# Moving four small loads from GpSimd's queue to ScalarE's, and draining GpSimd after each expert's outputs, in a gated linear attention with a routed mixture of experts

## The chip, the cores and the metric

The kernel runs on one core of one Trainium2 chip. The metric is device time in microseconds (us) of one execution, as the median of several executions. The engines are PE (TensorE), DVE (VectorE), ACT (ScalarE), POOL (GpSimd) and SP (SyncE). Each has an instruction stream of its own, and SP, ACT and POOL can also issue transfers (DMAs). In the views, "SPq" or "ACTq" is the instruction sequencer of that engine; a busy time is that of the engine itself, and the issuing of DMAs isn't counted in it.

## The reference

Two blocks follow each other. The first is a linear attention with complex gates: 4 batches, 8 heads, 768 steps, head width 48.

```python
mag = np.sqrt(a_re * a_re + a_im * a_im)
scale = np.minimum(mag, 0.999) / (mag + 1e-06)
a_re_n, a_im_n = (a_re * scale, a_im * scale)
for t in range(S):
    ar, ai = (a_re_n[:, :, t, :, None], a_im_n[:, :, t, :, None])
    new_re = ar * S_re - ai * S_im
    new_im = ar * S_im + ai * S_re
    kv = np.einsum('bhd,bhe->bhde', k[:, :, t], v[:, :, t])
    S_re, S_im = (new_re + kv, new_im)
    y[:, :, t] = np.einsum('bhd,bhde->bhe', q[:, :, t], S_re)
```

Its result, seen as 3072 tokens of width 384, goes through a router that picks one of 8 experts (hidden width 1024) for each token.

```python
logits = x @ w_gate
expert_idx = np.argmax(logits, axis=1)
...
for e in range(E):
    mask = expert_idx == e
    xe = x[mask]
    h = np.maximum(xe @ w1[e], 0.0)
    ye = h @ w2[e]
    out[mask] = gate_w[mask, None] * ye
```

## The kernel before

**Set-up.** POOL writes constants: the identity, counters, masks, and the tile `across` (line 231), which is cleared with a memset (line 232). Then four small DMAs on POOL's queue put the router's weights `w_gate` into parts of `across` (lines 235 and 236), and two POOL copies put identity blocks into other parts of it (line 237). POOL goes on with memsets of the unused rows of the tiles `st`, `xf`, `KX` and `QX`. PE multiplies by `across` at the end of each attention step, to turn the output and add the router's logits in one matmul.

**The gates.** For each batch the gates come in four pieces of four steps (`JQ`), as two DMAs each, real part and imaginary part, into the tile `big0`. So SP's queue begins with eight loads of 288 KB, in the order re, im, re, im and so on. For each piece the function `limit` (lines 405 to 437) applies the magnitude limit: ACT squares both parts (`Square`, line 414), DVE or PE adds them, ACT takes the logarithm and the exponential, and so on; ACT and DVE take turns, each waiting for the other's result. The function `front` then runs the recurrence on DVE, `fix` and `fold` make decayed queries and keys, and `attention` does the matmuls.

**The order.** All of this is first written as operations with costs. A planner (`in_time`) sorts them, and they are emitted in that order through `InOrder`, a wrapper that makes an engine keep the order in which the program was written. `P`, `V`, `A`, `T` and `Q` are such wrappers of POOL, DVE, ACT, PE and SP. ACT's stream begins with an activation-table load (line 294), a copy into `notes`, and the first `Square`.

**Completion semaphores.** Each DMA of SP or ACT signals on one of eight completion semaphores, which the framework gives out in turn in program order, whichever of the two queues issues it. A DMA that gets a semaphore again waits for the DMA that had it before. The first eight are those of the eight gate loads. POOL's DMAs have eight of their own.

**Routing.** After each batch the rows of x are written by indirect DMAs on POOL (line 788) into the DRAM buffer `sorted_x`, sorted by expert.

**The experts.** The loop of lines 894 to 937 goes over the eight experts. For each it loads up to 448 rows, multiplies by `w1` (24 matmuls), applies ReLU on ACT and DVE alternately, multiplies by `w2`, scales each block of 128 rows by its gate into a tile `yo` (three buffers), and the last 64 rows into `yh` (two buffers). The function `to_out` (lines 268 to 273) writes each with an indirect DMA on POOL into `out`: three blocks `yo` and one `yh` for most experts. The weights of expert e + 3 are fetched on SP's queue (line 933).

Of the kernel before, what the change touches and what calls it, by code (L numbers as in the profile page):

```python
# [17 lines left out]
B, H, S, D = 4, 8, 768, 48  # L18
N, DM, E, F = B * S, H * D, 8, 1024
# [13 lines left out]
XW = R2 + E  # L33
# [106 lines left out]
def gateloop_then_moe(ctx, tc, q, k, a_re, a_im, v, wg, w1, w2, out):  # L140
    nc = tc.nc
# [9 lines left out]
    def bc(ap, shape):  # L151
        return ap.to_broadcast(shape)
# [4 lines left out]
    def stt(o, a, s, b, op0, op1):  # L157
        nc.vector.scalar_tensor_tensor(out=o, in0=a, scalar=s, in1=b, op0=op0, op1=op1)
# [5 lines left out]
    P = InOrder(tc, nc.gpsimd)  # L164
# [6 lines left out]
    def blocks(e, u, a, z):  # L171

        return sorted_x[e * N + a:e * N + z, x_at(u)[0]:x_at(u)[0] + R2].rearrange("(c j) w -> j c w", j=32)
# [57 lines left out]
    across = consts.tile([128, H // 4, XW + E], FP32, name="across")  # L231
    P.memset(across, 0.0)
    for u in range(2):
        for n in range(2):
            P.dma_start(across[u * 64:u * 64 + D, :, (0 if n else XW):(E if n else XW + E)],
                        wg.rearrange("(m n u d) e -> u n d m e", n=2, u=2, d=D)[u, n])
        P.tensor_copy(across[u * 64:u * 64 + D, :, E + u * D:E + u * D + D],
                      bc(ident[u * 64:u * 64 + D, None, u * 64:u * 64 + D], [D, H // 4, D]))

# [20 lines left out]
    def fetch(e, queue):  # L260
        for w, at, n in ((w1, 0, DT * F), (w2, DT * F, FT * DM)):
            queue.dma_start(big[e % 3][:, at:at + n], w[e * 128:e * 128 + 128])

    def weights(e):
        w = big[e % 3]
        return w[:, 0:DT * F].rearrange("p (d f) -> p d f", f=F), w[:, DT * F:DT * F + FT * DM].rearrange("p (f d) -> p f d", d=DM)

    def to_out(y, rows, index):
        move = nc.gpsimd.indirect_dma_start(out=rows, out_offset=bass.IndirectOffsetOnAxis(ap=index, axis=0), in_=y,  # L269
                                            in_offset=None, bounds_check=rows.shape[0] - 1, oob_is_err=False).ins  # L270
        for other in outs:
            tc.declare_no_dep(move, other, reason="each token has a row of its own")
        outs.append(move)
# [17 lines left out]
    with ExitStack() as att:  # L291
# [401 lines left out]
        def early(weights_in):  # L693
# [28 lines left out]
            for i in range(EARLY // 128):  # L722
                o_ps, wait = (two[:, 0:DM], readers[0]) if i else (ps[7][:, 0:DM], used["at", 2])
                for f in range(FT):
                    o = pe(DM / 600 / 0.111, lambda i=i, f=f, o_ps=o_ps: T.matmul(o_ps, lhsT=ht[f][:, i * 128:i * 128 + 128], rhs=w2t[:, f, :],
                                                                                  start=(f == 0), stop=(f == FT - 1)),
                           [hts[f]] + ([o] if f else []), wait, first=B * G)
                o = act(DM, lambda i=i, o_ps=o_ps: A.activation(ys[i], o_ps, func=ACT.Copy, scale=gt_e[:, i, 0:1]), [o, state["early notes"]], free)
                pool_dma(1.1, lambda i=i: to_out(ys[i], out, to_e[:, i:i + 1]), [o, to])
# [122 lines left out]
    with ExitStack() as ms:  # L852
        xp = ms.enter_context(tc.tile_pool(name="xp", bufs=2))
        T = InOrder(tc, nc.tensor)
        TT, HALF = CAP // 128, DM // 2

        def notes_of(e):

            r = e * N
            gt = xp.tile([128, TT + 1, 2], FP32, name="gt")  # L860
            nc.sync.dma_start(gt[:, 0:TT, :], sorted_x[r:r + TT * 128, XD:].rearrange("(t p) w -> p t w", p=128))
            for u in range(2):
                nc.sync.dma_start(gt[u * 64:u * 64 + 64, TT, :], sorted_x[r + TT * 128:r + CAP, XD:])
            return gt

        def load(e):

            xq = xp.tile([128, CAP // 32, R2], FP32, name="xq")
            c0 = first_tile(e) * 4
            for u in range(4):  # L870
                nc.sync.dma_start(xq[u * 32:u * 32 + 32, c0:], blocks(e, u, c0 * 32, CAP))
            return xq, notes_of(e)

        def first_tile(e):
            return EARLY // 128 if e == 0 else 0

        def bank_of(kind):
            own = {"h": (2, 3, 4, 5), "o": (6, 7)}[kind]
            turn[kind] = turn.get(kind, -1) + 1
            return ps[own[turn[kind] % len(own)]]  # L880
        turn = {}

        def turned(e, xq):

            xt = mp.tile([128, DT, CAP], FP32, name="xt")
            for d in range(DT):
                c0 = first_tile(e) * 4
                nc.vector.transpose(xt[:, d, c0 * 32:].rearrange("p (c j) -> p c j", j=32), xq[:, c0:, d * 32:d * 32 + 32])  # L888
            return xt

        xq, gt = load(0)
        mp = ms.enter_context(tc.tile_pool(name="mp", bufs=2))
        xt = turned(0, xq)
        for e in range(E):
            if e + 1 < E:
                xq, gt_next = load(e + 1)
            w1t, w2t = weights(e)
            to = mp.tile([128, TT + 1], I32, name="to")
            t0 = first_tile(e)
            nc.vector.tensor_copy(to[:, t0:TT], gt[:, t0:TT, 1])  # L900
            stt(to[:, TT:TT + 1], gt[:, TT, 1:2], 2.0, upper, ALU.mult, ALU.add)
            ht = mp.tile([128, FT, CAP], FP32, name="ht")
            for f in range(FT):
                cols = slice(t0 * 128, CAP)
                h = bank_of("h")[:, cols]
                for d in range(DT):
                    T.matmul(h, lhsT=w1t[:, d, f * 128:f * 128 + 128], rhs=xt[:, d, cols], start=(d == 0), stop=(d == DT - 1))
                if f % 2:
                    nc.vector.tensor_scalar_max(ht[:, f, cols], h, 0.0)  # L909
                else:  # L910
                    nc.scalar.activation(ht[:, f, cols], h, func=ACT.Relu)  # L911
            if e + 1 < E:
                xt = turned(e + 1, xq)
            for i in range(t0, TT):
                o = bank_of("o")[:, 0:DM]
                for f in range(FT):
                    T.matmul(o, lhsT=ht[:, f, i * 128:i * 128 + 128], rhs=w2t[:, f, :], start=(f == 0), stop=(f == FT - 1))
                y = mp.tile([128, DM], FP32, name="yo", bufs=3)
                if i % 2:
                    nc.vector.tensor_scalar_mul(y, o, gt[:, i, 0:1])  # L920
                else:
                    nc.scalar.activation(y, o, func=ACT.Copy, scale=gt[:, i, 0:1])  # L922
                to_out(y, out, to[:, i:i + 1])
            o = bank_of("o")[:, 0:DM]
            for f in range(FT):
                for u in range(2):
                    T.matmul(o[u * 64:u * 64 + 64, 0:HALF], lhsT=ht[:, f, TT * 128:CAP], rhs=w2t[:, f, u * HALF:u * HALF + HALF],
                             start=(f == 0), stop=(f == FT - 1))
            y = mp.tile([128, HALF], FP32, name="yh", bufs=2)
            nc.vector.tensor_scalar_mul(y, o[:, 0:HALF], gt[:, TT, 0:1])  # L930
            to_out(y, halves, to[:, TT:TT + 1])
            if e + 3 < E:
                fetch(e + 3, nc.sync)
            if e == E - 2:
                n_gen = nc.values_load(trips[0:1, 0:1], min_val=0, max_val=1, skip_runtime_bounds_check_because="0 or 1")  # L935
            if e + 1 < E:
                gt = gt_next
# [176 lines left out]
```

## Time and profile before

| what | value |
|---|---|
| median of 5 executions | 665.64 us (664.05 to 668.29) |
| the profiled execution | 665.01 us, of which the span from first to last instruction is 663.3 us |
| PE busy | 548.9 us (83%) |
| DVE busy | 368.8 us (56%) |
| ACT busy | 289.5 us (44%) |
| POOL busy | 78.7 us (12%) |
| granted PE clock | 0.928 |

The span covers the instructions; the profiled execution's own time is 1.7 us longer. Shares of the whole span are averages over stages: the attention takes about the first 365 us, the experts the rest.

### The profile page before, as it was taken

The page shows a single profiled execution, that of the slowest core. Times are in us where ns is not written, and L with a number is a line of the kernel's source. Part 1 is how long each engine was busy: PE and PEld are TensorE (multiplying, and loading weights), DVE is VectorE, ACT ScalarE, POOL GpSimd, SP SyncE. Part 2 cuts the span into 40 slices and gives each one's busy share as a digit, 9 for nine tenths or more (in the row PEclk, how much of TensorE's full clock was granted, in tenths as well). Part 3 has the DMA queues.
Part 4 walks back from the last instruction along what each step waited for, and adds up shares of the span by engine and source line. Part 5 has one row for each costly group of instructions (what it writes and reads, how often), then busy time and mean ns, then how long its engine had stood idle before and what let it go on. Part 6 is the DMA issues. An engine that isn't in the chain of part 4 may idle for free. (4 is left out here: it accounts for less than half of the span.)

```text
span 663.3 us, 8204 instructions
## 1 busy us (share of the span) xinstructions
PE 548.9 (83%) x2594; PEld 336.2 (51%) x2594; DVE 368.8 (56%) x782; ACT 289.5 (44%) x940; POOL 78.7 (12%) x96
## 2 busy tenths in 40 slices
PE   1541388968899588968998999999999999999993
PEld 0220245645565355645566675555555555655552
DVE  5999999999999999999735121111111202010100
ACT  6555588688998688767743111010110100010100
POOL 9100000000004005003102110111101020101111
PEclk9865599989999588988999999999999999999998
DMA  9694856276724656078479434454554440100000
GB/s 258 151 247 116 193 161 175 79 194 163 192 70 125 185 153 183 29 180 203 113 274 398 89 132 121 139 141 138 151 139 136 116 126 30 37 6 24 9 12 29
DMA packets 77635, 89.81 MB, mean 135 GB/s; under 512 B 25341, under 2 KB 67343, under 8 KB 75536
## 3 DMA queue, kind: packets, MB, share of 16 engines
q1 hardware_dynamic: 74000, 79.33, 44.1%
q0 software_dynamic: 3584, 9.87, 4.2%
q8 instruction: 22, 0.36, 0.2%
q14 instruction: 29, 0.24, 0.1%
HBM read 54.31 MB, written 16.63 MB: 107 GB/s over the span
## 5 line engine op out<-in xcount | busy, mean ns | idle before, releaser
L136 PE MATMUL bank<-xt,big 128*128 128x448 f32 (+1 forms) x384 | 136.1, 515 | 1.1 <-DVE xt L888 1.1
L136 PE MATMUL bank<-big,ht 128*128 128x384 f32 (+1 forms) x608 | 136.8, 420 | 0.0
L136 PE MATMUL bank<-QX,KX 128*128 128x224 f32 (+1 forms) x384 | 96.0, 383 | 35.3 <-ACT QX L136 29.9
L136 PEld LDWEIGHTS bank<-big,ht 128*128 128x128 f32 (+1 forms) x608 | 84.7, 168 | 53.5 <-issue 6.9
L136 PEld LDWEIGHTS bank<-xt,big 128*128 128x128 f32 x384 | 71.3, 190 | 63.1 <-issue 60.8
L136 PEld LDWEIGHTS bank<-QX,KX 128*128 128x128 f32 x384 | 69.9, 209 | 52.0 <-issue 34.3
L909 DVE TENSOR_SCALAR ht<-bank 128x448 f32<-128x448 f32 (+1 forms) x32 | 18.9, 591 | 103.6 <-PE bank L136 103.6
L136 ACT ACTIVATE big<-big 128x576 f32<-128x576 f32 (+3 forms) x77 | 68.5, 902 | 15.5 <-DVE big L136 14.2
L136 ACT ACTIVATE QX<-diag,KX 96x48 f32<-96x48 f32 x280 | 72.4, 334 | 2.7 <-DMA KX<-pk 2.7
L911 ACT ACTIVATE ht<-bank 128x448 f32<-128x448 f32 (+1 forms) x32 | 16.5, 517 | 121.8 <-PE bank L136 121.8
L136 PE MATMUL two<-big,ident 128*128 128x512 f32 (+1 forms) x112 | 42.8, 538 | 29.7 <-ACT big L136 25.6
L788 POOL DMA_INDIRECT sorted_x<-xf,slot x24 | 29.8, 1242 | 316.6 <-DMA big<-in_a_im_dram 154.5
L136 PE MATMUL bank<-ak,vb 128*48 128x224 f32 (+1 forms) x384 | 54.2, 366 | 14.4 <-ACT ak L136 12.1
L136 DVE TENSOR_TENSOR big<-big,big 128x576 f32<-128x576 f32 (+3 forms) x86 | 65.0, 767 | 1.0 <-ACT big L136 0.2
L922 ACT ACTIVATE yo<-bank,gt 128x384 f32<-128x384 f32 x15 | 8.7, 580 | 122.4 <-PE bank L136 122.4
L136 DVE TENSOR_TENSOR big<-big 128x288 f32<-128x288 f32 (+5 forms) x108 | 55.2, 519 | 6.1 <-ACT big L136 5.3
L136 DVE TENSOR_TENSOR ak<-bank,causal 128x256 f32<-128x256 f32 x96 | 40.0, 419 | 17.1 <-PE bank L136 16.7
L269 POOL DMA_INDIRECT out_dram<-yo,to x22 | 21.3, 970 | 230.2 <-ACT yo L922 184.9
L136 PEld LDWEIGHTS two<-big,ident 128*128 128x128 f32 x112 | 22.6, 237 | 49.6 <-issue 32.6
L136 PE MATMUL bank<-QX,st 128*48 128x224 f32 (+1 forms) x320 | 43.5, 351 | 0.8 <-ACT st L136 0.8
L136 PE MATMUL bank<-across,ys 128*128 128x104 f32 x192 | 38.3, 291 | 4.7 <-ACT xf L136 2.3
L136 DVE TENSOR_TENSOR big<-big,carry 128x672 f32<-128x672 f32 x48 | 39.2, 853 | 0.1
(126 smaller groups left out, 548.7 us busy)
## 6 DMA issues: line engine op xcount, KB each, us to landing
big<-in_moe_w_dram SPq DMA_DIRECT2D x16, 1536.0 KB, 6.6
KX<-pk SPq DMA_DIRECT2D x44, 146.2 KB, 3.9
QX<-pk SPq DMA_DIRECT2D x44, 144.0 KB, 3.6
sorted_x<-xf SPq DMA_DIRECT2D x8, 731.5 KB, 6.5
xq<-sorted_x SPq DMA_DIRECT2D x28, 168.0 KB, 7.7
big<-in_a_re_dram SPq DMA_DIRECT2D x16, 288.0 KB, 3.3
big<-in_a_im_dram SPq DMA_DIRECT2D x16, 288.0 KB, 3.9
qt<-in_q_dram SPq DMA_DIRECT2D x12, 384.0 KB, 5.0
```

Source lines behind the costliest of these rows:

```text
L136: return lambda *a, **kw: self.tc.keep_in_program_order(f(*a, **kw))
L269: move = nc.gpsimd.indirect_dma_start(out=rows, out_offset=bass.IndirectOffsetOnAxis(ap=index, axis=0), in_=y, in_offset=None, bounds_chec ...
L788: move = nc.gpsimd.indirect_dma_start(out=sorted_x[:, :], out_offset=bass.IndirectOffsetOnAxis(ap=slot[:, i:i + 1], axis=0), in_=xfs[(b * ...
L909: nc.vector.tensor_scalar_max(ht[:, f, cols], h, 0.0)
L911: nc.scalar.activation(ht[:, f, cols], h, func=ACT.Relu)
L922: nc.scalar.activation(y, o, func=ACT.Copy, scale=gt[:, i, 0:1])
```

## The change

Two edits. The four loads of `w_gate` into `across` move from POOL's queue to ACT's, where they stand ahead of everything else that ACT does. And POOL gets a `drain` instruction behind the `yh` output of each of the experts 0 to 6. The outputs are now issued through `P`, so they keep program order on POOL.

```diff
@@ -232,8 +232,8 @@
     P.memset(across, 0.0)
     for u in range(2):
         for n in range(2):
-            P.dma_start(across[u * 64:u * 64 + D, :, (0 if n else XW):(E if n else XW + E)],
-                        wg.rearrange("(m n u d) e -> u n d m e", n=2, u=2, d=D)[u, n])
+            nc.scalar.dma_start(across[u * 64:u * 64 + D, :, (0 if n else XW):(E if n else XW + E)],
+                                wg.rearrange("(m n u d) e -> u n d m e", n=2, u=2, d=D)[u, n])
         P.tensor_copy(across[u * 64:u * 64 + D, :, E + u * D:E + u * D + D],
                       bc(ident[u * 64:u * 64 + D, None, u * 64:u * 64 + D], [D, H // 4, D]))
@@ -266,8 +266,8 @@
     def to_out(y, rows, index):
-        move = nc.gpsimd.indirect_dma_start(out=rows, out_offset=bass.IndirectOffsetOnAxis(ap=index, axis=0), in_=y,
-                                            in_offset=None, bounds_check=rows.shape[0] - 1, oob_is_err=False).ins
+        move = P.indirect_dma_start(out=rows, out_offset=bass.IndirectOffsetOnAxis(ap=index, axis=0), in_=y,
+                                    in_offset=None, bounds_check=rows.shape[0] - 1, oob_is_err=False).ins
@@ -929,6 +929,9 @@
             to_out(y, halves, to[:, TT:TT + 1])
+            if e < E - 1:
+
+                P.drain()
             if e + 3 < E:
                 fetch(e + 3, nc.sync)
```

The built program shows what this does to the instruction streams. The order of the work of PE, DVE, SP and POOL, and of ACT behind its first instructions, is as before. POOL's stream has the seven drains, with no wait of their own. ACT's stream now begins as follows, where each wait is for the completion semaphore of one of the eight gate loads, or for POOL's memset of `across`:

```
ACT 1  DMA across<-w_gate   waits for gate load 2 (im) and POOL's memset of across
ACT 2  DMA across<-w_gate   waits for gate load 4 (im)
ACT 3  DMA across<-w_gate   waits for gate load 5 (re)
ACT 4  DMA across<-w_gate   waits for gate load 7 (re)
ACT 5  activation-table load
ACT 6  copy into notes
ACT 7  Square of gate piece 1 (waits for gate load 1)
```

Before, instructions 5, 6 and 7 were the first three, and `Square` waited for the gate loads 1 and 2. On SP's queue the DMAs behind the gate loads have other completion semaphores than before, and so other earlier DMAs to wait for: the load of `kt_in` waits for gate load 3, the first of the six loads of `vb` for gate load 6 and the second for gate load 8 (before: 2, 3 and 4).

## The prediction

> **What bounds the kernel now.** I read first the table of busy time by stage, because shares of the whole span hide which engine is late where. Columns: stage, its length, then busy time and instruction count of PE, PE's weight loads, DVE, ACT and POOL, then granted clock, DMA share and GB/s.
>
> ```profile
> 0.00:16.60 16.60, 3.21 (x4) 1.50 (x5) 9.88 (x30) 10.59 (x16) 15.18 (x38) 1.00 0.91 258
> 100.00:200.00 100.00, 85.79 (x544) 56.53 (x541) 98.19 (x184) 87.93 (x307) 1.43 (x1) 0.97 0.56 147
> 200.00:300.00 100.00, 78.69 (x487) 51.25 (x486) 97.01 (x207) 76.27 (x281) 15.51 (x11) 0.86 0.52 141
> 400.00:663.00 263.00, 252.44 (x889) 141.23 (x888) 35.57 (x72) 22.98 (x42) 27.16 (x28) 0.99 0.29 82
> ```
>
> From about 100 to 300 us DVE has no room (98.19 and 97.01 of 100 us); among the experts PE has none (252.44 of 263). POOL is nowhere late, except that it is busy with memsets at the start. The first 16.6 us are different: no compute engine is full, so there a chain of waits sets the pace. So next I read ACT's timeline of the first 9 us (start, length, instruction, idle time before it and what ended that).
>
> ```profile
> 0.83 1.28 ACT L136 ACT_TABLE_LOAD   x1 [0.83 <-PEq L1103]
> 3.62 0.20 ACT L136 COPY notes<-token 128x6 f32<-128x6 f32 x1 [1.51 <-DVE token L219]
> 4.78 1.16 ACT L136 ACTIVATE big<-big 128x1152 f32<-128x1152 f32 x1 [0.96 <-DMA big<-in_a_im_dram]
> 6.77 0.77 ACT L136 ACTIVATE big<-big,w_bias 128x576 f32<-128x576 f32 x1 [0.82 <-DVE big L136]
> ```
>
> The first `Square` starts at 4.78, the moment gate load 2 is there. DVE's first use of it follows: DVE sits idle 2.24 us until `ACT big`, and starts at 5.98. After that ACT and DVE wait only for each other and for PE: among ACT's waits of the first 60 us the one of 1.0 us above is the only one on a DMA. So everything on ACT, DVE and PE behind it hangs on that 4.78.
>
> Third, SP's timeline of the same stretch, for the gate loads, and the DMA view taken around the issues of load 2 and of load 7 (last number: us from issue to landing).
>
> ```profile
> 1.34 0.49 SPq L136 DMA_DIRECT2D big<-in_a_im_dram  x1
> 2.42 0.51 SPq L136 DMA_DIRECT2D big<-in_a_im_dram  x1
> 2.97 0.51 SPq L136 DMA_DIRECT2D big<-in_a_re_dram  x1
> 4.36 1.78 SPq L136 DMA_DIRECT2D big<-in_a_re_dram  x1
> ```
>
> ```profile
> big<-in_a_im_dram SPq DMA_DIRECT2D x1, 288.0 KB, 3.4
> ```
>
> ```profile
> big<-in_a_re_dram SPq DMA_DIRECT2D x1, 288.0 KB, 6.7
> ```
>
> Load 2 landed at 1.34 + 3.4 = 4.7, which fits 4.78. Load 7 is issued at 4.36 and landed at 4.36 + 6.7 = 11.1. The loads between have no landing in this view; they were issued sooner.
>
> **The change, part by part.** *ACT's loads.* ACT now holds four DMAs ahead of its table load, and each waits on ACT's own stream. The first waits for load 2 (4.7; the memset of `across` ended at 3.17 + 0.33 = 3.5), the second and third for loads 4 and 5, the fourth for load 7: 11.1. Behind them stand the table load, the copy and the first `Square`, and so DVE's and PE's first work. The sum for the new start of `Square`:
> - fourth DMA may start at 11.1 (only this wait counts; loads 4 and 5 were issued 1.9 and 1.4 us before load 7, and their DMAs fit in between);
> - its issue: no DMA on ACT's queue is in the trace. Nearest rows: SP's gate loads take 0.45 to 1.78 us, median about 0.5; SP's small loads of `gt`, which have as few bytes, 0.49 to 2.83 with a median of 0.60; POOL's four loads of `across` themselves 0.56 to 0.79. I take 0.55, with 0.45 and 1.8 as ends. An issue at nothing isn't excluded either; it would take 0.55 off;
> - the table load 1.28, which before lay under the wait for `token` and cost nothing; that cover is gone;
> - the copy 0.20, of which I count 0.15, as ACT instructions overlap a little (the one at 8.88 takes 0.19 and the next starts at 8.97), and 0.1 for two hand-overs (4.7 to 4.78 is one).
>
> 11.1 + 0.55 + 1.28 + 0.15 + 0.1 = 13.2, against 4.78: **8.4 us later**. With 1.8 for the issue it is 9.6; with the issue at nothing, 7.8. Between the table load and the next ACT instruction the trace shows 1.51 us idle, given to `token`; the end of that wait (3.37 + 0.23 = 3.60) explains the next start. So any time that ACT needs behind a table load is bounded by 0 and 1.51, and the trace can't say more. I take 0, because the named releaser fits to 0.02 us, and keep 1.51 for the range: up to 11.1 in all.
>
> The Trainium skill ("ScalarE: Activation LUTs", section "What ACT_TABLE_LOAD costs") gives 1283 ns for the load, which this trace shows too, and puts a drain of 1380 ns behind it. By that rule the sum would be an estimated 9.8 us; no row here shows such a drain.
>
> *What the delay meets later.* A late start is made up only if some engine on the path waits, later, for something whose time does not hang on the first `Square`. Such things are the loads of q, k and v (SP issues them by 12.5, DVE multiplies by `qt` first at 63.5), the zeroing by POOL (its last memset starts at 18.1, first needed with the first `QX` at 64) and the `across` loads (PE first reads `across` at 85.8). All have 40 us and more to spare. Their cover is not touched: SP's loads of `kt_in` and `vb` now wait for other gate loads, at the latest load 8, issued at 6.18; even 4 us more leaves them 40 us early, and none of SP's later gate loads goes ahead of ACT's and DVE's progress anyway (the next one starts at 19.50). So I carry the whole 8.4 us to the end: at 98% busy DVE can't catch up.
>
> *What POOL saves.* Four DMA issues, 0.56 to 0.79 us each and about 2.5 us in all, so its memsets end about 2.7 us sooner. Nothing waits for them: 0.
>
> *Drains.* POOL's timeline among the experts:
>
> ```profile
> 470.83 0.97 POOL L269 DMA_INDIRECT out_dram<-yh,to  x1 [1.58 <-DVE yh L930]
> 494.43 0.97 POOL L269 DMA_INDIRECT out_dram<-yo,to  x1 [22.63 <-ACT yo L922]
> ```
>
> ```profile
> out_dram<-yh,to POOLq DMA_INDIRECT x8, 6.7
> ```
>
> A drain stands behind `yh`, and behind it the next expert's first `yo` is queued, which comes 22.6 us after. No drain is in the trace. Its bounds: nothing if it only waits for POOL's own pipe, and the landing of the output (6.7 us median, 9.9 the longest of all outputs) if it waits for that. A gain is excluded as it takes no work away. Even 9.9 leaves 12 us. So each of the seven costs 0; without the cover it would be up to 7 x 6.7 = 47 us. The last expert's outputs, which end the kernel, have none. `P` instead of the bare engine changes no order on POOL.
>
> The sum is made on the profiled execution: 665.01 + 8.4 = 673.4. That execution is 0.63 us under the median, so I forecast 665.64 + 8.4 = **674.0 us**.
>
> A second rule speaks the other way on the transfer itself: the skill ("DMA: Bandwidth & Descriptors", section "Issuing engine by pattern") sends simple loads to the hardware queues of SP or ACT, as generally faster than GpSimd's. By that rule alone the change would cost nothing, since these loads (5.0 us from issue to landing on POOL) are not waited for: 665.6. The row that decides is not the transfer's speed but what stands behind it on ACT.
>
> **The rivals.**
> - *Larger on ACT* (chance 0.2): the issue stalls as SP's did for load 7 (1.78), or ACT needs the 1.51 us behind the table load. 9.6 to 11.1 us later: 675.2 to 676.7. For it: SP's issue did stall just then, with eight loads on the way. Against it: by 11.1 seven of the eight have landed.
> - *Made up later, not slower* (0.08): ACT's late start is taken up by idle time in the opening of the attention. The place is the stretch 0 to 16.6, where DVE is busy only 9.88 and ACT 10.59 us; with all gate pieces landed, the two might overlap more. It decides if DVE reaches the end of `front` at the old time, for which DVE must win 8.4 us out of 6.7 idle ones. Then 665.6 us. Against it: those gaps are each other's results, in a fixed order, and no later gate load was waited for.
> - *Relieved POOL* (0.03): the memsets end 2.7 us sooner and something did wait for them: 663 at best, if ACT's waits cost nothing. No row shows such a waiter.
> - *Drains wait and are met* (0.04): POOL held up for more than 22.6 us behind a drain. From there each further us costs up to seven, 1 us over giving 681. The longest landing of an output is 9.9.
>
> **How the numbers follow.** My forecast case has 0.65 and gives 672.5 to 675: 7.8 to 8.4 us more, and about 1 us for the spread of medians, estimated from single executions between 664.05 and 668.29. The range takes in the larger case with half of that spread, up to 677.2; down to 671.2 it takes in a landing of load 7 that is 2 us sooner in other executions, and the spread. Left out are the last three cases, 0.15. A measurement of this kernel tells from no change about 0.5%, or 3.3 us: slower means over 669. The forecast, the larger case and the drains make 0.89 slower; made up later is the 0.08 of no difference; 0.03 remain for faster.
>
> **What would show it.** Right: in the changed profile ACT's table load starts near 11.7 instead of 0.83, the first `Square` near 13.2, DVE's first use of it near 14.4, and the same offset of about 8 us is seen in `qt`'s first use (63.5 before), in the first `yo` output (394.1) and at the end; POOL's gap before a `yo` stays near 22.6. Wrong: the offset shrinks on the way (then something absorbs it), the table load starts early, the four DMAs don't wait in order, or a `yo` output starts later than its data.

## The result, and the profile after

With both edits the kernel takes 668.4 us (median of 33 executions, 665.32 to 670.07), against 665.62 us before (59 executions): 2.8 us more, a ratio of 1.0036 (95% interval 1.0027 to 1.0045). The forecast was 674.0 us. The direction was right; the size was three times too large, and the time lies below the range. The profiled execution took 669.75 us, its span is 668.1 us.

ACT's timeline at the start, with the same columns as before:

```profile
4.73 6.00 ACTq L235 DMA_DIRECT2D across<-in_moe_w_gate_dram  x4
10.77 1.28 ACT L136 ACT_TABLE_LOAD   x1 [10.77 <-DMA big<-in_a_re_dram]
12.06 0.20 ACT L136 COPY notes<-token 128x6 f32<-128x6 f32 x1
12.16 1.16 ACT L136 ACTIVATE big<-big 128x1152 f32<-128x1152 f32 x1
```

The four loads hold ACT's sequencer from 4.73 to 10.73; the table load is released by a real part of the gates, which is load 7. The DMA view around the issue of load 7 (at 4.07) shows its landing 6.3 us later, at 10.4, and the view of line 235 shows what one issue costs on ACT's queue (min, median and max in ns):

```profile
big<-in_a_re_dram SPq DMA_DIRECT2D x1, 288.0 KB, 6.3
```

```profile
L235 ACTq DMA_DIRECT2D across<-in_moe_w_gate_dram x4: 318/318/394, 4.7 to 10.4; - x4
```

So `Square` starts at 12.16 instead of 4.78: 7.4 us late. Nothing makes that up on the way. The last `yh` on DVE, with which the computing ends, is at 652.48 before and at 661.79 after:

```profile
652.48 0.42 DVE L930 TENSOR_SCALAR yh<-bank,gt 128x192 f32<-128x192 f32 x1 [7.30 <-PE bank L136]
```

```profile
661.79 0.42 DVE L930 TENSOR_SCALAR yh<-bank,gt 128x192 f32<-128x192 f32 x1 [7.30 <-PE bank L136]
```

That is 9.3 us late, but the span is only 4.8 us longer. From this instruction to the end it is 10.8 us before and 6.3 us after: the kernel gained 4.5 us in its last 11 us. POOL's timeline before, which I had read, ends with the last output:

```profile
653.18 0.97 POOL L269 DMA_INDIRECT out_dram<-yh,to  x1 [1.58 <-DVE yh L930]
```

That is at 654.15, and the span ends at 663.3. My prediction took no account of the 9.2 us between. The view of the program's last line, under which its closing instructions stand, shows it, first before, then after (count, min/median/max in ns, first and last start):

```profile
L1110 POOLq DRAIN  x3: 46/108/4972, 657.5 to 663.0; - x3
```

```profile
L1113 POOLq DRAIN  x3: 46/103/378, 666.8 to 667.8; - x3
```

The long one of the three drains is the first; "the last drain" below is this one. Every program here ends with it. It took 4.97 us before, from 657.5 to 662.5, and takes 0.38 us after, 4.6 us less. The core's end waits for it: in the same view before, the next instructions of POOL's and of SP's sequencer start behind it.

```profile
L1110 POOLq EVENT_SEMAPHORE  x4: 17/17/17, 662.5 to 663.2; - x4
L1110 SPq EVENT_SEMAPHORE  x2: 17/17/17, 662.6 to 663.3; - x2
```

The seven new drains are in the view of POOL's other instructions, between 390 us and the end:

```profile
L136 POOLq DRAIN  x7: 2531/8918/10457, 405.8 to 625.8; - x7
```

They take 2.5 to 10.5 us each, and POOL's timeline shows that no output is late for them: the gap before the next `yo` is 22.62 us, before it was 22.63.

```profile
443.68 0.98 POOL L136 DMA_INDIRECT out_dram<-yh,to  x1 [1.57 <-DVE yh L930]
467.27 0.98 POOL L136 DMA_INDIRECT out_dram<-yo,to  x1 [22.62 <-ACT yo L922]
```

7.4 - 4.6 = 2.8 us is just what the medians show (the interval of the ratio is 1.8 to 3.0 us). The two profiles alone differ by 4.8 us, because between the first `Square` and the last `yh` one took 647.7 us and the other 649.6. In the ten profiles of this document the stretch takes 647.3 to 649.8 us, and short and long ones stand in both groups of kernels, with and without drains. So it goes with neither edit and looks like spread between executions; with one profile of each kernel that can't be shown.

### The profile page after: what moved, and what is told of

The parts are those of the page before. It is cut to its first block, busy times and chain, and to the rows that moved or that the text cites. A ratio compares the mean times of both kernels' runs of the same rounds, so it can differ in the third digit from the quotient of the medians.

```text
span 668.1 us, 8205 instructions
## 1 busy us (share of the span) xinstructions
PE 552.1 (83%) x2594; PEld 337.1 (50%) x2594; DVE 369.0 (55%) x782; ACT 289.2 (43%) x940; POOL 76.9 (12%) x92
## 5 line engine op out<-in xcount | busy, mean ns | idle before, releaser
L136 PE MATMUL two<-big,ident 128*128 128x512 f32 (+1 forms) x112 | 44.7, 556 | 37.0 <-ACT big L136 32.9
L136 PEld LDWEIGHTS bank<-across,ys 128*128 128x128 f32 x192 | 31.8, 207 | 15.5 <-ACT xf L136 4.8
```

What stands on the lines that cost most here:

```text
L136: return lambda *a, **kw: self.tc.keep_in_program_order(f(*a, **kw))
```

## The experiments

Theory: ACT's late start costs its full 7.4 us, and the drains take the work of the last drain to a place where POOL is idle. The main rival: the late start is mostly made up on the way, and the drains do nothing. Eight kernels were run, each in five rounds beside the kernel before, whose median was 665.59 us beside the first four and 665.96 us beside the others. The cuts of code are against the kernel before; those of the two kernels with one drain, and of the drain behind every output, are against the kernel with the drains alone, and that of the loads on SP against the changed kernel. `...` stands for what is left out.

**The loads on ACT alone**

```diff
-            P.dma_start(across[...], wg...)
+            nc.scalar.dma_start(across[...], wg...)
```

> Only the first edit: the four loads of across on ACT's queue, no drains. Theory A (ACT's late start costs its full 7.4 us, and the drains take about 4.6 us off the last drain of the program): first Square near 12.2 us as in the changed kernel, the program's last drain near 4.6 us (56 DMAs of POOL stand before it instead of 60), time 7.4 us over before, about 673.0. Rival B (ACT's late start is mostly made up in the attention, drains do nothing): 2 to 3 us over before, about 668.4, as with both edits.

Measured 671.95 us, a ratio of 1.0104 (1.0077 to 1.0131), which is 6.4 us between the medians and 6.9 by the ratio. In its profile `Square` starts at 11.81, 7.0 us late. The last drain:

```profile
L1110 POOLq DRAIN  x3: 40/103/4651, 664.1 to 669.4; - x3
```

4.65 us against the 0.05 + 56 x 0.082 = 4.64 expected. The time is 1.0 us under the expected 673.0: `Square` was 7.0 us late and not 7.4, and the sum had left out that the last drain gets 0.3 us shorter, which leaves 6.7. So the start is lost in full, as far as the interval tells (5.1 to 8.7 us); the rival, 668.4, falls.

**The drains alone**

```diff
-        move = nc.gpsimd.indirect_dma_start(...)
+        move = P.indirect_dma_start(...)
...
+            if e < E - 1:
+                P.drain()
```

> Only the second edit: the seven drains, the loads of across on POOL as before. Theory A: first Square at 4.8 us, the last drain 0.4 us instead of 4.97, time 4.6 us under before, about 661.0. Rival B (drains do nothing): 665.6, and a last drain near 5 us. Rival C (the shorter tail comes from the loads that left POOL's queue): the same 665.6.

Measured 660.58 us, a ratio of 0.9939 (0.9916 to 0.9962), 5.0 us between the medians. `Square` is at 4.95, the last drain takes 0.37 us:

```profile
L1113 POOLq DRAIN  x3: 46/108/373, 657.6 to 658.6; - x3
```

So the drains are worth about the 4.6 us that the last drain lost (4.1 by the ratio), and both rivals, at 665.6, fall. The two edits add up: +1.04% and -0.61% make +0.43%, and both together measured +0.36%.

**One drain, behind expert 6**

```diff
-            if e < E - 1:
+            if e == E - 2:
                 P.drain()
```

> Loads on POOL, one drain alone, behind the outputs of expert 6. If what a drain clears is counted in POOL's DMAs since the last drain (theory A1: 0.05 us + 0.082 us for each, from 4.97 us behind 60 and 0.38 behind 4): last drain 0.4 us, time 661.0 as with seven drains; the one inner drain takes at least 0.05 + 56 x 0.082 = 4.6 us. If it needs all seven (A2, each drain clears only its own share): last drain well over 2 us, time over 663.

Measured 660.59 us, 0.9924 (0.9899 to 0.9949). One drain does what seven do; A2 falls. The views of the inner and of the last drain:

```profile
L136 POOLq DRAIN  x1: 5855/5855/5855, 618.6 to 618.6; - x1
```

```profile
L1112 POOLq DRAIN  x3: 46/108/378, 659.6 to 660.6; - x3
```

The one inner drain takes 5.86 us, above the lower bound of 4.6.

**One drain, behind expert 0**

```diff
-            if e < E - 1:
+            if e == 0:
                 P.drain()
```

> Loads on POOL, one drain alone, behind the outputs of expert 0, so 28 DMAs of POOL follow until the last drain. Theory A1 (a price for each DMA since the last drain): last drain 0.05 + 28 x 0.082 = 2.35 us, time 2.6 us under before, about 663.0. Rival A3 (any earlier drain does all of it, as a first-use cost): last drain 0.4 us, 661.0.

Measured 664.09 us, 0.9965 (0.9943 to 0.9986); by the ratio 2.3 us less than before, by the medians 1.5. The last drain is the sharper reading:

```profile
L1112 POOLq DRAIN  x3: 46/108/2338, 659.8 to 662.7; - x3
```

2.34 us against 2.35 expected. So the last drain is not a first-use cost. It has a price for each DMA of POOL since the drain before. The outputs go through `P` here too, so it is the place of the drain that counts and not this wrapper.

**The table load ahead of the loads on ACT**

```diff
+    A0 = InOrder(tc, nc.scalar)
+    A0.preload_act_table_set("natural_log_exp_and_others")
...
-            P.dma_start(across[...], wg...)
+            A0.dma_start(across[...], wg...)
...
-        A.preload_act_table_set("natural_log_exp_and_others")
```

> The first edit alone, but with the activation-table load ahead of the four loads on ACT, where it lies under the wait for gate load 2. Theory A (the delay is a sum of the wait for gate load 7, one issue of 0.32, the uncovered table load of 1.28 and the copy): first Square near 10.8 us instead of 12.0, time 5.9 to 6.1 us over before, about 671.6; the last drain 4.64 us behind 56 DMAs. Rival (time beyond the table load's own 1.28 us stands behind it): the gain is 2.6 us, Square near 9.4.

Measured 671.32 us, 1.0083 (1.0070 to 1.0096). In the timeline the table load is back under the wait, and `Square` starts at 10.20:

```profile
0.83 1.28 ACT L136 ACT_TABLE_LOAD   x1 [0.83 <-PEq L1104]
4.83 5.22 ACTq L136 DMA_DIRECT2D across<-in_moe_w_gate_dram  x4
10.09 0.20 ACT L136 COPY notes<-token 128x6 f32<-128x6 f32 x1 [7.98 <-DMA big<-in_a_re_dram]
10.20 1.16 ACT L136 ACTIVATE big<-big 128x1152 f32<-128x1152 f32 x1
```

1.61 us sooner than with the loads alone. 1.28 of it is the table load; ACT's loads ended 0.33 sooner here (10.05 against 10.38). The rival's 2.6 isn't there. Over the kernel before beside each, the loads alone took 6.4 us more and this kernel 5.4, by the medians (6.9 and 5.5 by the ratios); the intervals overlap, so the times don't confirm the 1.28.

**One load of four on ACT**

```diff
-            P.dma_start(across[...], wg...)
+            (P if u or n else nc.scalar).dma_start(across[...], wg...)
```

> The first of the four loads on ACT, the other three on POOL, no drains. It waits only for gate load 2, which the first Square waits for in any case. Theory A (the waits for the later gate loads are the main price, not ACT's queue): first Square near 4.7 + 0.32 + 1.28 + 0.1 = 6.4 us, time 1.6 us over before, about 667.2. Rival D (a load on ACT's queue costs by itself, each a quarter of 7.4): about 1.9 from the queue plus the uncovered table load, Square near 8.0, 668.8. Last drain 0.05 + 59 x 0.082 = 4.9 us.

Measured 667.33 us, 1.0021 (1.0008 to 1.0033), 1.4 us between medians. ACT's timeline:

```profile
4.84 0.39 ACTq L235 DMA_DIRECT2D across<-in_moe_w_gate_dram  x1
5.26 1.28 ACT L136 ACT_TABLE_LOAD   x1 [5.26 <-DMA big<-in_a_im_dram]
6.66 1.16 ACT L136 ACTIVATE big<-big 128x1152 f32<-128x1152 f32 x1
```

`Square` starts at 6.66: the wait for load 2, which it has anyway, then one issue and the table load. So a load on ACT's queue costs little by itself; the waits for later gate loads make most of the 7.4. The last drain takes 4.89 us behind 59 DMAs (4.9 expected).

**The loads on SP, with the drains**

```diff
-            nc.scalar.dma_start(across[...], wg...)
+            nc.sync.dma_start(across[...], wg...)
```

> The loads of across on SP's queue, behind the gate loads and the load of qt; the seven drains as in the change. Theory A: nothing that is needed soon stands behind them on SP, so first Square at 4.8 us, last drain 0.4 us, time as with the drains alone, 660.6. Rival (the four waits on SP hold up loads that matter): over 662.

Measured 661.05 us, 0.9927 (0.9914 to 0.9941). `Square` at 4.86, last drain 0.38 us. SP's timeline has the four loads behind the load of `qt`:

```profile
7.79 1.78 SPq L235 DMA_DIRECT2D across<-in_moe_w_gate_dram  x4
```

They are issued in one run, from 7.79 to 9.57, so no wait held them up for long there. They cost nothing that the times can tell, and what stands behind them on SP isn't needed for some 50 us. Which of the two spares the time, the short waits or what stands behind, this run doesn't separate.

**A drain behind every output of experts 0 to 6**

```diff
                 to_out(y, out, to[:, i:i + 1])
+                if e < E - 1:
+                    P.drain()
```

> Loads on POOL; a drain behind every output of experts 0 to 6, those behind a yo followed by the next output 2.6 to 5.2 us later, so the cover is much smaller. If a drain ends about 0.2 us after the landing of the output before it (theory A, landings of yo about 2.6 us): the yh output of each expert starts up to 0.6 us late, nothing on PE waits for it, time as with seven drains, 660.6. If drains hold POOL longer than the gaps: yo buffers run out, PE waits, over 662.

Measured 660.91 us, 0.9928 (0.9915 to 0.9941). The time is as expected, but the drains are longer than I thought. POOL's timeline of one expert:

```profile
431.97 0.97 POOL L136 DMA_INDIRECT out_dram<-yo,to  x1 [4.20 <-ACT yo L922]
436.67 0.97 POOL L136 DMA_INDIRECT out_dram<-yh,to  x1 [3.74 <-issue]
```

The `yh` output starts after 3.74 us of idle time instead of 1.58, so 2.2 us late and not 0.6. PE doesn't wait for it: 20.48 us of idle time follow before the next `yo` (at 458.12). On DVE the small copies of line 900 do wait longer for outputs to land, 9.6 us in two places against 2.9 in one before, but DVE has room among the experts.

The quickest kernels are those with a drain behind expert 6 and without loads on ACT, 660.6 to 661.1 us; the runs don't separate them. They beat both the kernel before and the changed one.

## Why the prediction was right or wrong

**What bounds the kernel: right at the start, blind at the end.** The first `Square` does set the pace of all that follows. But I read the stages by busy time, which counts no drain, and so took the 9.2 us behind the last output as nothing.

**ACT's loads: right in mechanism, a little large.** The order, the waits and the end of the table load's cover were as I said. Forecast 8.4 us, measured 7.4. Load 7 landed at 10.4 instead of 11.1 (it was issued 0.3 us sooner and took 0.4 less), an issue took 0.32 instead of 0.55, and the copy with its hand-overs took 0.1 less than the 0.25 that I had put down. The issue was faster than every one of the rows I took as bounds (0.45 to 2.83), but within the bound of nothing that I had kept.

**The time behind a table load: 0 was right.** The copy starts at 12.06, and the load ends at 10.77 + 1.28 = 12.05. The 1380 ns of drain that the Trainium skill ("ScalarE: Activation LUTs", section "What ACT_TABLE_LOAD costs") puts behind it are not there; the measurement decides. The same page's 1283 ns for the load itself fits.

**Carrying the delay to the end: right.** With the loads alone the time rose by 6.4 to 6.9 us, for a start 7.0 us late and a last drain 0.3 us shorter. The rival "made up later" would have been near 665.6 and is refuted.

**The drains: this step failed.** I wrote "No drain is in the trace" and "A gain is excluded as it takes no work away". Both were wrong. The trace had one at the end, of 4.97 us, directly on the path, in a part of the profile that I hadn't read. And a drain that takes no work away can still move it. What I said of the new drains themselves held: each waits for the landing of the output before it, inside the cover of 22.6. They take 8.4 to 10.5 us behind experts 0 to 4, up to 0.6 past the 9.9 that I had as the end, and 2.5 to 2.9 behind experts 5 and 6. Only behind experts 0 to 4 are later weights fetched, which fits, but no run shows that the fetch is the reason. The missing -4.6 us is what put the time below the range; 665.6 + 8.4 - 4.6 would have been 669.4, and with the measured 7.4 it is the 668.4 found. That the direction was right owes nothing to my account of the drains: 7.4 happens to be more than 4.6.

**The rivals.** The larger delay on ACT, the relieved POOL and the drains that are met did not occur: ACT's issues were short (0.32 to 0.39 us), the memsets of POOL ended sooner and no one waited, and even 26 drains delayed no matmul enough to be seen. None of my rivals was a gain from the drains.

The Trainium skill ("DMA: Bandwidth & Descriptors", section "Issuing engine by pattern") names Sync for a simple load, calls the queues of Sync and Scalar generally faster, and says nothing of what stands behind the load in its queue. Here the four loads cost 6.4 us on ACT and nothing to be seen on SP. No run shows a faster transfer either: the landings that the profiles hold took 4.7 and 5.8 us on ACT's queue, and 5.0 at the median on POOL's.

## What to carry to other kernels

Before you move a small load to another queue, list what it will wait for there and what stands behind it; a load that nobody needs yet can hold up the first instruction that everybody needs. Read the last microseconds of the trace as closely as the first: drains and final waits count in no busy time, and work that they leave to the end can be moved under an idle stretch. When two edits come together, predict and run them apart, since their effects can partly cancel, as +7.4 and -4.6 us did here.

## What the runs showed of the hardware

A drain of POOL takes time for each DMA that POOL issued since the drain before, even when all have landed: in the kernel before the last output landed at 656.4, and the last drain ran from 657.5 to 662.5. The last drain took 0.38 us behind 4 DMAs, 2.34 behind 28, 4.65 behind 56, 4.89 behind 59 and 4.97 behind 60: 0.05 + 0.082 us for each. The four direct loads of 3 KB count like the indirect outputs of up to 128 rows (4.97 - 4.65 = 0.32 for four).

A drain right behind an output also waits until that output has landed. In the kernel with the drains alone, the outputs `yh` issued at 543.81 and 580.27 landed after these times:

```profile
out_dram<-yh,to POOLq DMA_INDIRECT x1, 7.0
```

```profile
out_dram<-yh,to POOLq DMA_INDIRECT x1, 2.4
```

so at 550.8 and 582.7. Their drains took

```profile
L136 POOLq DRAIN  x1: 7457/7457/7457, 543.6 to 543.6; - x1
```

```profile
L136 POOLq DRAIN  x1: 2846/2846/2846, 580.0 to 580.0; - x1
```

and ended at 551.1 and 582.8, 0.2 us behind the landing. The twelve drains of this kernel and of the changed one that stand behind four DMAs all ended 0.15 to 0.25 us behind it. With more DMAs to clear it takes longer. The first drain of this kernel stands behind 32:

```profile
out_dram<-yh,to POOLq DMA_INDIRECT x1, 7.4
```

```profile
L136 POOLq DRAIN  x1: 8978/8978/8978, 396.6 to 396.6; - x1
```

The output was issued at 396.79 and landed at 404.2, and the drain ended at 405.6, 1.4 us later. In the changed kernel, behind 28, it is 1.2 us, and the one inner drain behind 56, whose output landed 2.1 us after its issue, ended 3.5 us later. So part of the price is paid while the drain waits for the landing; how much, the runs don't show. What POOL does in the 0.082 us for each DMA, the runs don't show.
